# Cosine attention and a GELU feed-forward block on one core: attention passes of the next batch moved ahead of the w_in stage, with new filler portions and five more start-up spins

## The chip, the core and the metric

The kernel runs on one core of a Trainium2 chip. The metric is the device time of one launch in microseconds (us). A core has TensorE (PE, matrix multiplication; its weight loads are listed as PEld), VectorE (DVE), ScalarE (ACT), GpSimd (POOL) and SyncE (SP), which only issues transfers. Each takes its instructions in the order in which the kernel's code emits them, and semaphores tie the engines together. Matrix products land in PSUM, which has eight banks of 2 KB a partition, and have to be copied or consumed from there by DVE or ACT.

## What is computed

Attention on normalised q and k, for 8 batches of 12 heads, 448 positions and 64 channels, then two matrix products with a GELU between them:

```python
q_n = q / (norm(q) + 1e-6);  k_n = k / (norm(k) + 1e-6)
scores = q_n @ k_n.T / tau                     # tau = 0.1
attn = softmax(scores);      o = attn @ v      # per batch and head
x = o laid out as (8 * 448) x 768
out = gelu_exact(x @ w_in) @ w_out             # 768 -> 2048 -> 768
```

## The kernel before

**Stages.** For each batch b the program emits an attention stage, `attention(b, fill)` from line 600 on (batch 0 has its own, written out instruction by instruction, `attention_first`, line 411), and then the w_in stage `first(b)` (line 652): 96 matmuls `hp` (line 664) of 448 columns, each group of six followed by a GELU on ACT (line 699). The w_out product of a batch is not a stage of its own. It is cut into *fillers*, single matmuls of 384 columns (`second_pieces`, line 343), which are put between the parts of the next batch's attention. Sixteen fillers make a *piece*: they accumulate into one PSUM bank, and behind the last one DVE copies the bank to SBUF (`ot`, line 356); two pieces make a tile of the output that SyncE stores. A stage of an odd batch gets 96 fillers (six pieces), that of an even batch 128 (eight). What is left after the last batch runs at the end.

**Attention.** The 12 heads of a batch are three *quads* of four heads. A quad has seven key chunks, so a batch has 21 *passes*. A pass is four matmuls of 64 x 64 tiles that run side by side in the array (`st`, `scores`, line 246) and one exp on ACT over their result (`pt`, `exps`, line 253). `visit(b, pairs)` emits the next passes of batch b; its numbers say which of the three two-bank *pair* buffers of PSUM each pass uses. When a quad's seven passes are there, `both(g, p)` (line 325) emits its sums (`sm`, line 275, 16 matmuls), then DVE's chain that turns, adds, inverts and spreads the sums (lines 297, 309, 312, 314, 318), its values (`o`, line 289, 28 matmuls, into pair buffer p), and two multiplications on DVE that write x (line 323).

**Banks.** Two single PSUM banks, mm0 and mm1, serve everything else. `mm_tile` (line 99) hands out the bank that `turn` names and flips `turn`; each filler piece takes one that way at its first matmul. Sums ask with `aside=0`, which takes the bank that `turn` names without flipping it. A new owner of a bank waits until the old one's content has been read.

**Norms of later quads.** The squares of q and k run on GpSimd (line 156), their reduction `nq` on DVE (line 165), the logarithm and the root on ACT (lines 172 and 181), then a small addition on GpSimd, the reciprocal on DVE and the scaling of q and k on GpSimd (line 208). For batches from 1 on a DMA transposes the scaled q and k (line 220). `upto(f, n)` emits whatever of step f is not yet emitted up to number n. In an attention stage one reduction, for a quad of the next batch, is emitted between the first and the second quad's `both` (line 635); in batch 7 there is no such quad left.

**Order of a stage, batches 3 to 7.** `run()` emits the next portion of the fillers. With six portions, (16, 14, 16, 18, 16, 16) or (20, 18, 20, 22, 32, 16), the order is: fillers, 3 passes, fillers, 3, fillers, 3, fillers, 3, sums and values of quad 0, 2 passes, the reduction, fillers, 3 passes, sums and values of quad 1, 2 passes, fillers, sums and values of quad 2, 2 passes of the next batch. The w_in stage follows; its first two matmul groups use mm0 and mm1, the next four use pair buffers 0 and 1.

**Start.** `spin(n)` (line 406) emits n matmuls whose result nobody reads.

Of the kernel before, what the change touches and what calls it, by code (L numbers as in the profile page):

```python
# [16 lines left out]
def kernel(  # L17
# [18 lines left out]
    B, H, S, D = q.shape  # L36
# [163 lines left out]
    def scale(u, parts=None):  # L200
        g, s0, s1 = units[u]
        n, j = place[u]
        rn = rn_t[n][:, j]
        if g not in qkb_t:
            qkb_t[g] = qkbp.tile([128, 2, C, 2, D], BF16, tag="qkb", name=f"qkb{g}")
        qkb, t = qkb_t[g], qk_t[g]
        for eng, i in parts or ((nc.gpsimd, 0), (nc.gpsimd, 1)):
            eng.tensor_tensor(  # L208
                qkb[:, i, :, s0:s1].rearrange("p c s d -> p s c d"), t[:, i, s0:s1],
                rn[:, i].to_broadcast([128, s1 - s0, C, D]), ALU.mult)  # L210
# [3 lines left out]
    def transposes(u, i=None):  # L214
        g, s0, s1 = units[u]
        qkb = qkb_t[g]
        if g not in qkT_t:
            qkT_t[g] = qkTp.tile([128, 2, C, 128], BF16, tag="qkT", name=f"qkT{g}")
        if i is None:
            nc.sync.dma_start_transpose(out=qkT_t[g].rearrange("p i c s -> p (i c) s"),  # L220
                                        in_=qkb.rearrange("p i c s d -> p (i c s d)"))
            return
        tp = tp_t[u, i] = mm_tile(f"tp{u}_{i}", (128, C, 128), BF16)
        for c in range(C):
            nc.tensor.transpose(tp[64 * s0:64 * s1, c, :], qkb[:, i, c, s0:s1].rearrange("p s d -> p (s d)"), ident)  # L225
# [33 lines left out]
    def sums(g, chunks=range(C)):  # L259
        for c in chunks:  # L260
            if c == 0:
                bank_t[g, "sm"] = ps_acc.tile([128, 512], F32, tag="sm", name=f"sm{g}") if g < NQ else \
                    mm_tile(f"sm{g}", aside=0)
            for s in range(2):
                if g < NQ:
                    nc.tensor.matmul(bank_t[g, "sm"][64 * s:64 * (s + 1), :S],  # L266
                                     lhsT=ones2.rearrange("p a h r -> p (a h r)"), rhs=pt_t[g, s, c],
                                     start=(c == 0), stop=(c == C - 1), tile_position=(0, 64 * s))
                    continue

                half = 2
                for i in range(2) if c == half else ((c - (c > half)) % 2,):
                    r = 32 * (2 * s + i)
                    cols = slice(i * S // 2, (i + 1) * S // 2) if c == half else slice(0, S)
                    nc.tensor.matmul(bank_t[g, "sm"][r:r + 32, cols], lhsT=ones, rhs=pt_t[g, s, c][:, cols],  # L275
                                     start=(c < 2), stop=(c >= C - 2), tile_position=(0, r))

    def values(g, chunks=range(C), p=None):
        for c in chunks:
            if c == 0 and g < NQ:  # L280
                bank_t[g, 0] = ps_acc.tile([128, 512], F32, tag="o", name=f"o{g}_0")
                bank_t[g, 1] = mm_tile(f"o{g}_1")
            elif c == 0:
                o = pair(p, f"o{g}")
                bank_t[g, 0], bank_t[g, 1] = o[:, 0], o[:, 1]
            for s in range(2):
                for h in range(2):
                    rows, cols = slice(64 * h, 64 * (h + 1)), slice(64 * s, 64 * (s + 1))
                    nc.tensor.matmul(bank_t[g, h][cols, :S], lhsT=v_t[g][rows, s, c, :],  # L289
                                     rhs=pt_t[g, s, c][rows], start=(c == 0), stop=(c == C - 1),  # L290
                                     tile_position=(64 * h, 64 * s))
# [3 lines left out]
    def turned(g):  # L295
        tr = rcp.tile([128, NB, 32], F32, tag="tr", name=f"tr{g}")
        nc.vector.transpose(tr.rearrange("p b r -> p (b r)"), bank_t.pop((g, "sm"))[:, :S])  # L297
        bank_t[g, "tr"] = tr.rearrange("p b (k r) -> p k b r", k=2)

    def inverted(g):  # L300
        tr = bank_t.pop((g, "tr"))
        if g < NQ:
            su = tr[:, :, :, 0]
        else:


            for j in range(4):
                o = j ^ 1
                nc.vector.tensor_reduce(tr[32 * j:32 * (j + 1), :, :, 1], tr[32 * o:32 * (o + 1), :, :, 0:1],  # L309
                                        mybir.AxisListType.X, ALU.add)  # L310
            su = rcp.tile([128, 2, NB], F32, tag="su", name=f"su{g}")
            nc.vector.tensor_reduce(su, tr[:, :, :, 0:2], mybir.AxisListType.X, ALU.add)
        rc = bank_t[g, "rc"] = rcp.tile([128, 2, NB], F32, tag="rc", name=f"rc{g}")
        nc.vector.reciprocal(rc, su)

    def spread(g, h):
        rs = rcp.tile([128, NB, 32], F32, tag=f"rs{h}", name=f"rs{g}_{h}")
        nc.vector.transpose(rs, bank_t[g, "rc"][:, h].to_broadcast([128, NB, 32]))  # L318
        rs_t[g, h] = rs.rearrange("p b r -> p (b r)")

    def normalise(g, h):
        b, n = divmod(g, NQ)
        nc.vector.tensor_tensor(x_t[b][:, 2 * n + h, :], bank_t.pop((g, h))[:, :S], rs_t.pop((g, h)), ALU.mult)  # L323

    def both(g, p):
        sums(g)
        turned(g)
        inverted(g)
        spread(g, 0)
        spread(g, 1)  # L330
        values(g, p=p)
        normalise(g, 0)
        normalise(g, 1)
# [66 lines left out]
    def upto(f, n, last=None):  # L400
        last = {load_qk: NG, load_v: NV, root: len(groups), load_wi: NQ + 1, load_wo: 4}.get(f, NU)
        while done.get(f, 0) < min(n, last):
            done[f] = done.get(f, 0) + 1
            f(done[f] - 1)

    def spin(n):
        ps = ps_mm.tile([128, 512], F32, tag=f"mm{turn[0]}", name="spin")
        for _ in range(n):
            nc.tensor.matmul(ps[:, :S], lhsT=ident, rhs=blank, start=True, stop=True)  # L409

    def attention_first():
# [19 lines left out]
        reduce(2, Q)  # L431
        roots(1)
        scale(0, ((GP, 0),))
        spin(2)
        transposes(0, 1)
        square(2, ((AC, K),))
        inverses(1)
        spin(1)
        transposes(0, 0)
        square(3, ((AC, Q),))  # L440
        copies(0, 1)
# [2 lines left out]
        square(3, ((AC, K),))  # L444
        scale(1, ((GP, 1),))
        upto(load_qk, 5)
        spin(1)
        transposes(1, 0)
        reduce(2, K)
        scores(0, ((0, 0), (0, 1)))  # L450
# [8 lines left out]
        inverses(2)  # L459
        copies(1, 1)  # L460
        exps(0, ((0, 2), (0, 3)))
        spin(2)
        scores(0, ((0, 4), (0, 5)))
        scale(2, ((GP, 0),))
        reduce(3, Q)
# [127 lines left out]
    def visit(b, pairs):  # L593
        for p in pairs:
            n, c = passes[at.get(b, 0)]
            at[b] = at.get(b, 0) + 1
            scores(b * NQ + n, ((0, c), (1, c)), p)
            exps(b * NQ + n, ((0, c), (1, c)))

    def attention(b, fill):  # L600
        fill = list(fill)
        if len(fill) == 128:
            parts = iter((20, 18, 20, 22, 32, 16))
        else:
            parts = iter((20, 13, 14, 17, 16, 16) if b == 1 else (16, 14, 16, 18, 16, 16))

        def run():
            for _ in range(next(parts)):
                fill.pop(0)()

        x_t[b] = xp.tile([128, KD, S], BF16, tag="x", name=f"x{b}")
        g0, u = b * NQ, b * NQ + 1
        run()
        upto(scale, u + 3)
        upto(transposes, u + 3)
        if b == 1:
            upto(load_qk, g0 + NQ + 2)
            upto(square, u + 4)
        visit(b, (0, 1, 2))
        if b > 1:  # L620
            upto(scale, u + 4)
            upto(transposes, u + 4)
        run()
        visit(b, (0, 1, 2))
        run()
        upto(load_qk, g0 + NQ + 3)
        visit(b, (0, 1) if b <= 2 else (0, 1, 2))
        upto(square, u + 5)
        run()
        visit(b, (0, 1, 2))  # L630
        both(g0, 0)
        upto(load_v, b + 3)
        upto(load_qk, g0 + NQ + 4)
        visit(b, (1, 2))
        upto(reduce, u + 4 + (b > 1))
        run()
        visit(b, (1, 2, 0))
        both(g0 + 1, 1)
        visit(b, (2, 0))
        n = 2 * b + 5 + (b > 1)  # L640
        if n < len(groups):
            logs(n)
            roots(n)
        run()
        both(g0 + 2, 2)
        if n < len(groups):
            inverses(n)
            done[root] = n + 1
            if b > 1:
                visit(b + 1, (0, 1))  # L650

    def first(b):
        sb, hf = divmod(b, 2)
# [77 lines left out]
    fill = []  # L731
    for b in range(B):
# [12 lines left out]
        fill = [f for t, ni in todo if t not in tail for f in second_pieces(sb, t, ni)]  # L745
# [38 lines left out]
```

## Time and profile before

The time is 414.46 us, the median of three runs (414.1 to 420.34); the profiled execution has a span of 412.4 us.

| What | PE | PE weight loads | DVE | ACT | POOL |
|---|---|---|---|---|---|
| busy, us | 405.6 | 211.8 | 188.3 | 248.8 | 168.1 |
| share of the span | 98% | 51% | 46% | 60% | 41% |

Some costly groups of instructions, from the page:

| Group | Count | Mean ns of one |
|---|---|---|
| ACT exp `pt`, L253 | 168 | 916 |
| PE filler `op`, L352 | 864 | 326 |
| PE `hp`, L664 | 768 | 353 |
| PE scores `st`, L246 | 672 | 358 |
| PE values `o`, L289 | 672 | 352 |
| PE sums `sm`, L275 | 336 | 332 |
| DVE reduction `nq`, L165 | 30 | 1635 |
| DVE copy `ot`, L356 | 54 | 547 |

The page and the views name each row by line, engine and operation, and by the names of the tiles it writes and reads (`op<-wo,g`: writes op from wo and g). "x16" is a number of instructions merged into one row. Times in a timeline are us from the start of the span; brackets hold the idle time of that engine ahead of the row and what ended it. Consecutive matmuls overlap in the array, and their listed ends are modelled, so the distance from one start to the next says more than a listed length.

In the trace the attention stage of batch 3 takes 27.6 us (149.11 to 176.68), that of batch 4 32.8 us (194.85 to 227.63), and a w_in stage 18.2 us (176.68 to 194.85).

### The profile page before, as it was taken

The page shows a single profiled execution, that of the slowest core. Times are in us where ns is not written, and L with a number is a line of the kernel's source. Part 1 is how long each engine was busy: PE and PEld are TensorE (multiplying, and loading weights), DVE is VectorE, ACT ScalarE, POOL GpSimd, SP SyncE. Part 2 cuts the span into 40 slices and gives each one's busy share as a digit, 9 for nine tenths or more (in the row PEclk, how much of TensorE's full clock was granted, in tenths as well). Part 3 has the DMA queues.
Part 4 walks back from the last instruction along what each step waited for, and adds up shares of the span by engine and source line. Part 5 has one row for each costly group of instructions (what it writes and reads, how often), then busy time and mean ns, then how long its engine had stood idle before and what let it go on. Part 6 is the DMA issues. An engine that isn't in the chain of part 4 may idle for free.

```text
span 412.4 us, 8272 instructions
## 1 busy us (share of the span) xinstructions
PE 405.6 (98%) x3503; PEld 211.8 (51%) x3503; DVE 188.3 (46%) x380; ACT 248.8 (60%) x364; POOL 168.1 (41%) x117
## 2 busy tenths in 40 slices
PE   7999999999999999999999999999999999999996
PEld 3445555555555555555555555555555555555564
DVE  5785316931278222933158331773128611481021
ACT  6996696477556567665664658646665457754300
POOL 4996665094900928053720628227360233000000
PEclk9999999999999999999999999999999999999999
DMA  8999999852495507944496332965088120610033
GB/s 287 260 258 213 203 204 303 188 132 48 83 243 164 135 0 115 251 102 120 36 216 200 79 94 52 226 176 134 2 151 212 38 46 0 122 40 2 0 78 77
DMA packets 66484, 54.53 MB, mean 132 GB/s; under 512 B 38672, under 2 KB 62352, under 8 KB 66448
## 3 DMA queue, kind: packets, MB, share of 16 engines
q1 hardware_dynamic: 54464, 41.79, 39.7%
q0 software_dynamic: 11600, 11.80, 18.2%
q8 instruction: 27, 0.44, 0.4%
q10 hardware_dynamic: 384, 0.43, 0.3%
q14 instruction: 9, 0.07, 0.1%
HBM read 45.61 MB, written 11.01 MB: 137 GB/s over the span
## 4 chain that ended last, share of the span: by engine, by line
PE 96%; DMA 2%; SPq 1%; ACT 1%; issue 0%; DVE 0%
PE hp L664 35%; PE op L352 35%; PE st L246 10%; PE o L289 8%; PE sm L275 4%; DMA qk<-in_k_dram 2%; PE op L371 1%; PE sm L266 1%; PE tp L225 1%; SPq L129 1%; PE spin L409 0%; ACT sq L154 0%; ACT pt L253 0%; DVE last L374 0%; ACT root L178 0%
## 5 line engine op out<-in xcount | busy, mean ns | idle before, releaser
L253 ACT ACTIVATE pt<-st 128x896 bf16<-128x896 f32 x168 | 142.5, 916 | 65.4 <-PE st L246 65.1
L352 PE MATMUL op<-wo,g 128*128 128x384 bf16 x864 | 148.0, 326 | 0.0
L664 PE MATMUL hp<-x,wi 128*128 128x448 bf16 x768 | 146.9, 353 | 0.0
L352 PEld LDWEIGHTS <-g 128*128 128x128 bf16 x864 | 81.5, 98 | 62.2 <-issue 10.8
L664 PEld LDWEIGHTS <-wi 128*128 128x128 bf16 x768 | 74.4, 98 | 71.4 <-issue 3.0
L699 ACT ACTIVATE g<-hp 128x448 bf16<-128x448 f32 x128 | 65.5, 545 | 67.7 <-PE hp L664 67.5
L208 POOL TENSOR_TENSOR qkb<-qk,rn 128x896 bf16<-128x896 f32 (+1 forms) x50 | 80.3, 1632 | 41.1 <-DVE rn L192 41.1
L165 DVE TENSOR_REDUCE nq<-sq 128x28 f32<-128x1792 f32 (+2 forms) x30 | 48.7, 1635 | 51.4 <-POOL sq L156 47.7
L356 DVE COPY ot<-op 128x384 f32<-128x384 f32 x54 | 29.6, 547 | 88.2 <-PE op L352 86.1
L156 POOL TENSOR_TENSOR sq<-qk 128x1792 f32<-128x1792 f32 (+1 forms) x22 | 66.6, 3039 | 5.1 <-DMA qk<-in_k_dram 5.1
L190 POOL TENSOR_SCALAR se<-sr 128x28 f32<-128x28 f32 (+1 forms) x16 | 4.8, 298 | 124.4 <-ACT sr L181 124.2
L246 PE MATMUL st<-qkT 64*64 64x448 bf16 x672 | 47.8, 358 | 0.2 <-ACT pt L253 0.2
L289 PE MATMUL o<-pt,v 64*64 64x448 bf16 x672 | 37.2, 352 | 0.0
L192 DVE RECIPROCAL rn<-se 128x28 f32<-128x28 f32 (+2 forms) x20 | 7.1, 357 | 57.5 <-POOL se L190 57.3
L246 PEld LDWEIGHTS <-qkT 64*64 64x64 bf16 x672 | 18.3, 105 | 23.0 <-issue 14.8
L318 DVE STREAM_TRANSPOSE rs<-rc 128x448 f32<-128x448 f32 x48 | 28.2, 623 | 0.8
L323 DVE TENSOR_TENSOR x<-o,rs 128x448 bf16<-128x448 f32 x48 | 27.1, 598 | 0.3
L289 PEld LDWEIGHTS <-v 64*64 64x64 bf16 x672 | 17.8, 106 | 16.7 <-issue 8.1
L297 DVE STREAM_TRANSPOSE tr<-sm 128x448 f32<-128x448 f32 x24 | 15.5, 647 | 13.4 <-PE sm L275 11.1
L275 PE MATMUL sm<-pt,ones 128*32 128x448 bf16 (+1 forms) x336 | 17.8, 332 | 0.0
L309 DVE TENSOR_REDUCE tr<-tr 32x28 f32<-32x28 f32 x84 | 16.4, 196 | 1.6
L275 PEld LDWEIGHTS <-ones 128*32 128x32 bf16 x336 | 6.8, 96 | 9.0 <-issue 7.2
(43 smaller groups left out, 120.6 us busy)
## 6 DMA issues: line engine op xcount, KB each, us to landing
qk<-in_q_dram SPq DMA_DIRECT2D x23, 448.0 KB, 6.2
qk<-in_k_dram SPq DMA_DIRECT2D x23, 448.0 KB, 8.6
out_dram<-ot SPq DMA_DIRECT2D x48, 192.0 KB, 3.7
v<-in_v_dram POOLq DMA_DIRECT2D x7, 672.0 KB, 12.8
wo<-in_moe_w_out_dram POOLq DMA_DIRECT2D x4, 768.0 KB, 12.4
wi<-in_moe_w_in_dram POOLq DMA_DIRECT2D x4, 512.0 KB, 14.1
out_dram<-ot SPq DMA_DIRECT2D x12, 96.0 KB, 2.2
wi<-in_moe_w_in_dram POOLq DMA_DIRECT2D x4, 256.0 KB, 14.1
```

The source lines that it names most:

```text
L156: eng.tensor_tensor(sq[:, part], t[:, part], t[:, part], ALU.mult)
L165: nc.vector.tensor_reduce(nq[:, part], sq[:, part], mybir.AxisListType.X, ALU.add)
L208: eng.tensor_tensor(qkb[:, i, :, s0:s1].rearrange("p c s d -> p s c d"), t[:, i, s0:s1], rn[:, i].to_broadcast([128, s1 - s0, C, D]), ALU. ...
L246: nc.tensor.matmul(st[cols, n, :S], lhsT=qkT[rows, 1, c, cols], rhs=qkT[rows, 0, :, cols], start=True, stop=True, tile_position=(64 * s, 6 ...
L253: nc.scalar.activation(pt[:, :m], st[:, :m, :S], AF.Exp, scale=inv_tau)
L275: nc.tensor.matmul(bank_t[g, "sm"][r:r + 32, cols], lhsT=ones, rhs=pt_t[g, s, c][:, cols], start=(c < 2), stop=(c >= C - 2), tile_position ...
L289: nc.tensor.matmul(bank_t[g, h][cols, :S], lhsT=v_t[g][rows, s, c, :], rhs=pt_t[g, s, c][rows], start=(c == 0), stop=(c == C - 1), tile_po ...
L318: nc.vector.transpose(rs, bank_t[g, "rc"][:, h].to_broadcast([128, NB, 32]))
L352: nc.tensor.matmul(ps[:, :NH], lhsT=g_t[sb][:, kf, t * 128:(t + 1) * 128], rhs=wo[:, kf, ni * NH:(ni + 1) * NH], start=(kf == 0), stop=(kf ...
L356: nc.vector.tensor_copy(ot[:, ni * NH:(ni + 1) * NH], ps[:, :NH])
L664: nc.tensor.matmul(hps[m], lhsT=wi[:, kd, m * 128:(m + 1) * 128], rhs=x_t[b][:, kd, :], start=(kd == 0), stop=(kd == KD - 1))
L699: nc.scalar.activation(g_t[sb][:, m, hf * S:(hf + 1) * S], hps.pop(m), AF.Gelu)
```

## The change

From batch 3 on, five passes of a batch (not two) are emitted in the stage before it: three ahead of the sums and values of the last quad, two behind them. They are to give ACT work ahead of the w_in stage and to take three passes out of the following attention stage, whose fillers are then handed out in five portions instead of six. Batches 1 and 2 keep their portions. In the first batch five more spins are emitted, at four places, where PE would be waiting for other engines.

```diff
@@ attention_first
         scale(0, ((GP, 0),))
-        spin(2)
+        spin(4)
         transposes(0, 1)
...
         inverses(1)
-        spin(1)
+        spin(2)
         transposes(0, 0)
...
         upto(load_qk, 5)
-        spin(1)
+        spin(2)
         transposes(1, 0)
...
         exps(0, ((0, 2), (0, 3)))
-        spin(2)
+        spin(3)
         scores(0, ((0, 4), (0, 5)))
@@ attention(b, fill)
-        if len(fill) == 128:
-            parts = iter((20, 18, 20, 22, 32, 16))
+        if b <= 2:
+            parts = iter((20, 13, 14, 17, 16, 16) if b == 1 else (20, 18, 20, 22, 32, 16))
         else:
-            parts = iter((20, 13, 14, 17, 16, 16) if b == 1 else (16, 14, 16, 18, 16, 16))
+            parts = iter((26, 26, 26, 25, 25) if len(fill) == 128 else (20, 19, 19, 19, 19))
...
         upto(load_qk, g0 + NQ + 3)
-        visit(b, (0, 1) if b <= 2 else (0, 1, 2))
+        if b <= 2:
+            visit(b, (0, 1))
+            run()
         upto(square, u + 5)
-        run()
         visit(b, (0, 1, 2))
         both(g0, 0)
...
         run()
+        if 1 < b < B - 1:
+            visit(b + 1, (2, 0, 1))
         both(g0 + 2, 2)
         if n < len(groups):
             inverses(n)
             done[root] = n + 1
-            if b > 1:
-                visit(b + 1, (0, 1))
+        if 1 < b < B - 1:
+            visit(b + 1, (0, 1))
```

## The prediction

> **What bounds the kernel now.** I read the page first: the busy shares, then the chain that ended last.
>
> ```profile
> PE 405.6 (98%) x3503; PEld 211.8 (51%) x3503; DVE 188.3 (46%) x380; ACT 248.8 (60%) x364; POOL 168.1 (41%) x117
> ...
> PE 96%; DMA 2%; SPq 1%; ACT 1%; issue 0%; DVE 0%
> ```
>
> TensorE (PE) is 98% busy and is 96% of the chain; no other engine comes near. A busy share can hide waits, so I next read the timeline of PE for the batch with a short filler list (batch 3) and took start-to-start distances.
>
> ```profile
> 162.00 0.76 PE L246 MATMUL st<-qkT 64*64 64x448 bf16 x12
> 162.69 0.85 PE L275 MATMUL sm<-pt,ones 128*32 128x448 bf16 x16
> 163.46 1.52 PE L289 MATMUL o<-pt,v 64*64 64x448 bf16 x28
> 164.81 0.59 PE L246 MATMUL st<-qkT 64*64 64x448 bf16 x8
> 165.33 2.77 PE L352 MATMUL op<-wo,g 128*128 128x384 bf16 x16
> 168.04 0.76 PE L246 MATMUL st<-qkT 64*64 64x448 bf16 x12
> 168.73 0.85 PE L275 MATMUL sm<-pt,ones 128*32 128x448 bf16 x16
> ```
>
> Columns: start, length, instruction, count. Three passes (st x12) take 0.69 us to the next start, sums 0.77 to 0.78, values 1.35, two passes 0.52. Filler blocks (op) of 14, 16, 18 and 20 take 2.38, 2.70, 3.03 and 3.35 us: 0.1625 us a matmul and 0.10 us once per block. No block takes longer than its like anywhere from batch 3 on: PE waits for nothing there. So the time is PE's work plus whatever waits the change brings. Where could it wait? The next view is the timeline of VectorE (DVE) beside the same stretch.
>
> ```profile
> 162.10 0.56 DVE L356 COPY ot<-op 128x384 f32<-128x384 f32 x1 [2.04 <-PE op L352]
> 163.59 0.65 DVE L297 STREAM_TRANSPOSE tr<-sm 128x448 f32<-128x448 f32 x1 [0.93 <-PE sm L275]
> 164.27 0.82 DVE L309 TENSOR_REDUCE tr<-tr 32x28 f32<-32x28 f32 x4
> ...
> 166.83 1.11 DVE L323 TENSOR_TENSOR x<-o,rs 128x448 bf16<-128x448 f32 x2
> 167.87 2.00 DVE L165 TENSOR_REDUCE nq<-sq 128x28 f32<-128x1792 f32 x1
> 169.79 0.54 DVE L356 COPY ot<-op 128x384 f32<-128x384 f32 x1
> 170.26 0.63 DVE L297 STREAM_TRANSPOSE tr<-sm 128x448 f32<-128x448 f32 x1
> ```
>
> After the first quad's sums DVE works without a pause: the quad's chain (transpose to x) ends 5.18 us after the sums began at 162.69, then the reduce of the squares, and only then the copy that empties a filler piece: 7.10 us after the sums' start, done at 7.64. That piece's last matmul was over at about 168.0; its copy came 1.8 us late, because DVE takes its instructions in program order. It does no harm here, since the sums of the second quad (168.73) go into the bank of the piece before, which the copy at 162.10 had emptied.
>
> **What the Trainium skill says.** "Perfetto Trace Analysis", Identifying the Most-Contended Engine: matmul busy time doesn't tell how close PE is to its peak. The trace agrees: a filler matmul is listed at some 326 ns, but the starts are 162.5 ns apart, hence my use of starts. "TensorE: Matmul & The Clock Gate", Back-to-back issue gap: N/2.4 + 2.5 ns at full clock; that is 162.5 ns for 384 columns and 189 for 448, both as in the trace (hp: 18.17 us for 96). Same page, Architectural detail: VectorE and ScalarE are strictly first in, first out; the late copy above agrees. Same page, What's actually happening: after an idle window of about 3.4 us the PE clock falls to half. In the trace the spins' starts are 373 ns apart until 5.2 us and 189 ns after, and the granted clock stays full to the end of the matmuls.
>
> **The change part by part.**
>
> 1. Spins: five more matmuls at four places, 0.19 us each (5.43 to 5.62 in the trace), 0.95 us if all lay on the path. At line 434 two more (0.38) fall into an idle 0.81 before the transposes, which wait for GpSimd. At 447 one falls into an idle 0.20, again before GpSimd's scaling. At 462 the scores at 13.71 wait for an exp, with 0.15 idle; three spins from 13.01 and 0.10 for the change of shape end at 13.68. At 438 one has no room and pushes a transpose by some 0.06, which the next wait for GpSimd (0.20) takes up. I take 0; bounds 0 to 0.95.
>
> 2. Passes moved. The count stays 21 a batch. From batch 3 to 7 the block of passes between fillers goes and its two neighbouring filler parts join: one block less, 0.10 each, -0.50 us. Three passes stand ahead of the last quad's sums in batches 2 to 6: a block of 0.69, of which 0.56 is work taken from the next batch and 0.13 the change of tile shape. It replaces the block that went, so only batch 2 gains one (+0.13) and batch 7 loses one (-0.13). Sum -0.5 us. ScalarE's exps: five in a row need 5 x 0.81 = 4.1 us while PE is busy for 3.3 (0.69 + 0.78 + 1.35 + 0.48) and then 1.5 us on two other banks in the w_in stage, and the pair buffers are asked for in the order already used around the first quad, where nothing waits. Cost 0. Inputs: the third quad's transposed q and k must be there 13.9 us into the stage; the DMA transpose issued at 156.27 landed at 160.28, 11.2 us in. Cost 0.
>
> 3. Filler parts, and here I see a new wait. Fillers come as pieces of 16 matmuls, alternating between two banks; a piece's first matmul waits for the copy of the piece two before. Sums take the bank that the next piece would take: that of the piece before the current one. Before, the first quad's sums stand at filler 64 (short list) or 80 (long), both whole pieces, so the copy of the last piece goes ahead of the DVE chain. After, they stand at 20+19+19 = 58 and 26+26+26 = 78: a piece is cut, it ends just behind the sums, and its copy falls behind DVE's chain and the reduce, at 7.10 to 7.64 us after the sums' start.
>
> Short list (batches 3, 5): piece 4 ends 6 matmuls behind. The next quad's sums stand at filler 77, in piece 5, so they want piece 4's bank. They are due after 0.78 + 1.35 + 0.52 + (19 x 0.1625 + 0.10 = 3.19) + 0.69 = 6.53 us; the bank is free at 7.64 + 0.05 for the hand-over (from an exp's end to the scores at 13.71: 0.05). Wait 1.16 us.
>
> Long list (batches 4, 6): piece 5 ends 2 behind, piece 6 16 later, and piece 7 wants piece 5's bank. It is due after 0.78 + 1.35 + 0.52 + 18 x 0.1625 = 5.58 us. In batch 4 before, where PE's timeline has the first quad's sums at 211.03, DVE's has the reduce in the same place:
>
> ```profile
> 216.22 2.00 DVE L165 TENSOR_REDUCE nq<-sq 128x28 f32<-128x1792 f32 x1
> 218.14 0.54 DVE L356 COPY ot<-op 128x384 f32<-128x384 f32 x1
> ```
>
> The copy begins 7.11 after the sums and ends at 7.65; wait 7.65 + 0.05 - 5.58 = 2.12 us. Behind the waiting matmul stand all of PE's later matmuls, and nothing else can fill in, since PE takes them in order. Batch 7 has no reduce (no quad left to prepare): its copy ends at 5.18 + 0.54 = 5.7, before 6.53. Batch 2 keeps its old parts. After the wait DVE catches up: the next copies end at least 0.8 us before their banks are asked for.
>
> Sum of the waits: 2 x 1.16 + 2 x 2.12 = 6.6 us. With -0.5 and the spins at 0: 414.46 + 6.1 = **420.5 us**.
>
> **Rivals.** No wait: if the copy came ahead of the reduce or the banks alternated otherwise, only -0.5 would be left: 413.9 us, not slower than before. For it speaks that PE waits nowhere now; against it, the copy at 169.79 behind the reduce, and the sums at 168.73 not waiting for that copy, which is just the bank rule above. Chance 0.13. More waits: in batches 2 and 7, or for spins on the path (+0.95) and one DMA transpose late by 2 us, since transposes landed up to 8.8 us after issue: 423.5 us, chance 0.07. Clock: a wait of 2.1 us that counts as an idle window would bring 3.4 us at half speed, an estimate by the clock-gate page, 1.7 us each in four places: 427 us; against it, the wait is shorter than that window. Chance 0.05. My forecast has 0.75.
>
> **How the numbers follow.** The forecast alone moves little: DVE's order is measured twice, so its waits may be off by some 0.3 us each, and spins by up to 0.95. The range of 417.5 to 423.0 holds it, one of the four waits missing or halved, and part of the third case; left out are the first rival, the clock and the rest of the third, some 0.2. Slower by over 2% is over 422.8 us: 0.10. Faster by 2% would be under 406.2, which no case reaches: 0.01. Within 2%: 0.89.
>
> **What would show it.** In PE's timeline of batches 3 and 5 the passes ahead of the second quad's sums last about 1.2 us longer; in 4 and 6 the filler block of 25 takes 6.3 instead of 4.16 us; among the waits PE appears behind DVE's copy, four times, 6 to 7 us in all. The reduce of line 165 stands right before each late copy. Batch 7 shows none. I am wrong if these blocks have their usual lengths, or if the wait is for an exp or a DMA.

## The result, and the profile after

The changed kernel takes 421.83 us (median of six executions), the kernel before beside it 414.75. The ratio is 1.0173, with a 95% interval of 1.0152 to 1.0194: slower by some 7 us, within the stated range of 417.5 to 423.0, and 1.3 us over the forecast of 420.5. The ratio leaves out two executions of the kernel before, of 420.34 and 420.95 us; later ones like them, of kernels that wait for no copy, have a mean granted clock of 0.983 to 0.987, and no trace shows where they lost it.

The page of the changed kernel, busy shares and the chain that ended last:

```profile
PE 408.5 (97%) x3508; PEld 213.7 (51%) x3508; DVE 188.1 (45%) x380; ACT 249.0 (59%) x364; POOL 168.1 (40%) x117
...
PE 92%; DVE 6%; issue 1%; DVEq 0%
```

The span grew by 8.0 us (412.4 to 420.4), but PE's busy time only by 2.9. PE's work is nearly the same, and DVE, which had 0% of the chain, has 6% of it now. The timeline of PE for batch 3 (columns as before; the brackets give the idle time ahead of the row and what ended it):

```profile
164.54 3.26 PE L352 MATMUL op<-wo,g 128*128 128x384 bf16 x19
167.73 0.76 PE L246 MATMUL st<-qkT 64*64 64x448 bf16 x12
169.60 0.85 PE L275 MATMUL sm<-pt,ones 128*32 128x448 bf16 x16 [1.11 <-DVE ot L356]
```

and for batch 4:

```profile
214.61 3.10 PE L352 MATMUL op<-wo,g 128*128 128x384 bf16 x18
219.67 1.30 PE L352 MATMUL op<-wo,g 128*128 128x384 bf16 x7 [1.96 <-DVE ot L356]
```

In batch 3 the second quad's sums start 1.87 us after the passes ahead of them instead of 0.69: a wait of 1.18 us for the copy `ot`. In batch 4 the filler block of 25 breaks after its 18th matmul and lasts 6.29 us instead of 4.17: a wait of 2.12. DVE's timeline of batch 3 shows what stood ahead of that copy:

```profile
162.80 0.65 DVE L297 STREAM_TRANSPOSE tr<-sm 128x448 f32<-128x448 f32 x1 [2.55 <-PE sm L275]
...
166.05 1.12 DVE L323 TENSOR_TENSOR x<-o,rs 128x448 bf16<-128x448 f32 x2
167.09 2.00 DVE L165 TENSOR_REDUCE nq<-sq 128x28 f32<-128x1792 f32 x1
169.01 0.54 DVE L356 COPY ot<-op 128x384 f32<-128x384 f32 x1
```

The sums began at 161.90; the copy starts 7.11 us later and ends at 169.55, and PE's next sums start at 169.60. Cutting the trace at the starts of the attention stages (the view of given stretches: start and end, length, then the busy time and number of instructions of PE, PEld, DVE, ACT and POOL, then the granted PE clock, that is, the share of full speed at which PE was allowed to run, and last the DMA share and GB/s) gives the whole account:

```profile
97.77:150.09 52.32, 52.32 (x462) 27.42 (x461) 24.70 (x47) 33.74 (x48) 20.82 (x12) 1.00 0.50 123
150.09:196.91 46.82, 45.71 (x410) 23.85 (x408) 22.28 (x44) 29.71 (x43) 20.82 (x12) 1.00 0.54 130
196.91:249.91 53.00, 51.04 (x442) 26.97 (x440) 23.30 (x46) 29.71 (x43) 20.82 (x12) 1.00 0.51 122
249.91:296.73 46.82, 45.71 (x410) 23.85 (x409) 22.27 (x44) 29.71 (x43) 20.82 (x12) 1.00 0.54 130
296.73:351.26 54.53, 52.57 (x441) 27.21 (x440) 21.25 (x45) 29.71 (x43) 17.69 (x11) 0.97 0.39 85
351.26:395.83 44.57, 44.57 (x389) 23.25 (x388) 15.91 (x40) 24.97 (x36) 3.62 (x3) 1.00 0.17 38
```

Before, the same stretches (attention and w_in stage of batches 2 to 7) are 51.58, 45.74, 50.95, 45.74, 50.95 and 45.37 us long, and PE is busy through all of each. The "predicted" column adds up the terms of the prediction.

| Batch | Before, us | After, us | Measured | Predicted |
|---|---|---|---|---|
| up to batch 2's start | 97.53 | 97.77 | +0.24 | 0 |
| 2 | 51.58 | 52.32 | +0.74 | +0.69 |
| 3 | 45.74 | 46.82 | +1.08 | +1.06 |
| 4 | 50.95 | 53.00 | +2.05 | +2.02 |
| 5 | 45.74 | 46.82 | +1.08 | +1.06 |
| 6 | 50.95 | 54.53 | +3.58 | +2.02 |
| 7 | 45.37 | 44.57 | -0.80 | -0.79 |

Five stages are within 0.05 us of the prediction. Batch 6 takes 1.53 us more than batch 4, which has the same work, and a mean granted clock of 0.97. These short stretches around its wait show why:

```profile
317.51:320.92 3.41, 1.45 (x12) 0.72 (x14) 2.38 (x3) 0.00 (x0) 0.00 (x0) 1.00 1.01 356
320.92:324.33 3.41, 3.41 (x40) 1.19 (x36) 0.91 (x3) 2.54 (x3) 0.00 (x0) 0.50 0.51 144
```

For 3.41 us behind the wait PE ran at half its clock. Four of the six executions have a mean granted clock of 0.994 or 0.995, which is about one such stretch (half of 3.41 us is 0.4% of 420), and take 421.79 to 422.21 us; the two at 1.0 take 420.66 and 420.96. The waits by themselves therefore give about the forecast, and a clock drop in most executions adds 1.2 us. Of the six, only the profiled one has a trace; for the other five the number of drops is read from the mean clock.

### The profile page after: what moved, and what is told of

It reads as the page before. It is cut to its first block, busy times and chain, and to the rows that moved or that the text cites. A ratio compares the mean times of both kernels' runs of the same rounds, so it can differ in the third digit from the quotient of the medians.

```text
span 420.4 us, 8269 instructions
## 1 busy us (share of the span) xinstructions
PE 408.5 (97%) x3508; PEld 213.7 (51%) x3508; DVE 188.1 (45%) x380; ACT 249.0 (59%) x364; POOL 168.1 (40%) x117
## 2 busy tenths in 40 slices
DMA packets 66484, 54.53 MB, mean 130 GB/s; under 512 B 38672, under 2 KB 62352, under 8 KB 66448
## 4 chain that ended last, share of the span: by engine, by line
PE 92%; DVE 6%; issue 1%; DVEq 0%
PE hp L667 35%; PE op L352 31%; PE st L246 9%; PE o L289 7%; PE sm L275 4%; PE spin L409 2%; DVE nq L165 2%; PE op L371 1%; PE sm L266 1%; PE tp L225 1%; DVE tr L309 1%; DVE x L323 1%; DVE rs L318 1%; DVE tr L297 1%; DVE ot L356 0%
```

## The experiments

The theory is that PE waits for filler copies that the new portions put behind DVE's chain and the reduction, and that the longer wait can set off a clock drop. Rival P says that the passes moved ahead cost the time themselves. Rival S puts a good part of it at the start, on the spins. A piece is called cut where the sums stand inside it, and whole where they stand at its end.

### The spins alone

```diff
 # the kernel before
-        spin(2)
+        spin(4)
         transposes(0, 1)
...
 # and the three other places of the change
```

> The kernel before with the five added spins alone. Theory (the added time is the wait for a late copy, plus a clock drop that the wait sets off): the spins cost 0 to 0.4 us, so 414.4 to 414.9; 0.4 where the clock comes up late and the 24 spins reach past the scaling that the first transposes wait for. Rival S (a good part of the added 7 us lies at the start): 415.5 or more.

Measured: 414.68 us, ratio 1.0005 (0.9995 to 1.0014). A cost of up to 0.6 us is all that this allows; it can't be told from none. Rival S falls. The trace of the changed kernel shows how the spins can get onto the path: there the clock became full at 6.89 us, not 5.22, so the first 24 spins were slower, and the transposes started behind them at 9.33, while GpSimd's scaling had ended at 8.67. Two spins fewer would have freed PE 0.38 us earlier. In the trace with the spins alone the clock became full at 5.68, and the transposes followed the scaling (8.76) at 8.82, so there the first spins cost nothing. That execution is the slowest of its fifteen (417.81 us); it lost its time later on, where PE waited 1.17 us for a copy on DVE and 1.72 us for an exp on ACT, which had itself waited 2.28 us for a transfer of k.

### Cut pieces in the kernel before

```diff
 # the kernel before, in attention
-        if len(fill) == 128:
+        if b > 2:
+            parts = iter((20, 18, 20, 20, 25, 25) if len(fill) == 128
+                         else (16, 14, 16, 12, 19, 19))
+        elif len(fill) == 128:
             parts = iter((20, 18, 20, 22, 32, 16))
```

> The kernel before with the filler portions alone changed, from batch 3 on: (16, 14, 16, 12, 19, 19) and (20, 18, 20, 20, 25, 25), so that the sums stand at fillers 58 and 77, or 78 and 103, as in the changed kernel. Passes and spins as before. Theory: the same four waits, 2 x 1.17 and 2 x 2.12 us, in all 6.6: 421.0 us, and 1.7 more in an execution with a clock drop. Rival P: 414.5, since the passes are where they were.

Measured: 421.98 us (median of four), ratio 1.0180 (1.0160 to 1.0201). The profiled execution took 420.9 and shows the four waits without a clock drop; the others have clocks of 0.995 and 0.996 and take 421.7 to 422.9. From the view of the waits (us in total, times, longest us):

```profile
PE op L352 <- DVE ot L356: 3.9, 2, 2.0
PE sm L275 <- DVE ot L356: 2.2, 2, 1.1
```

The stages of batches 3 to 6 grew by 1.15, 2.12, 1.14 and 2.12 us, 6.5 together; those of 2 and 7 did not change. Nothing but the portions differs from the kernel before, so moving the passes isn't needed for the loss: rival P falls as its cause.

### The reduction behind the copies

```diff
 # the changed kernel
-        upto(reduce, u + 4 + (b > 1))
+        if b <= 2:
+            upto(reduce, u + 4 + (b > 1))
         run()
+        upto(reduce, u + 4 + (b > 1))
```

> The changed kernel with the reduction of the squares emitted behind the filler portion that follows the first quad, so that it stands behind the copies on VectorE, for batches 3 to 6. The cut pieces stay. Theory: the copy ends 5.72 us after the sums began; no wait in batches 3 and 5 (due at 6.53), 0.2 us in 4 and 6 (due at 5.58); no clock drop; 414.3 to 415.0 us. Rival P, or a rival in which the cut pieces cost by themselves: about 421.

Measured: 414.24 us, ratio 0.9997 (0.9986 to 1.0008). The cut pieces, the passes ahead and the new spins are all still there; only the place of the reduction in DVE's order is another. DVE's timeline of batch 4:

```profile
214.91 1.12 DVE L323 TENSOR_TENSOR x<-o,rs 128x448 bf16<-128x448 f32 x2
215.95 1.14 DVE L356 COPY ot<-op 128x384 f32<-128x384 f32 x2
217.01 2.01 DVE L165 TENSOR_REDUCE nq<-sq 128x28 f32<-128x1792 f32 x1
219.36 0.65 DVE L297 STREAM_TRANSPOSE tr<-sm 128x448 f32<-128x448 f32 x1 [0.34 <-PE sm L275]
```

The copies now end before the reduction, which ends before the next sums are done. PE's timeline of the same stretch:

```profile
213.40 4.44 PE L352 MATMUL op<-wo,g 128*128 128x384 bf16 x25
217.77 0.76 PE L246 MATMUL st<-qkT 64*64 64x448 bf16 x12
```

The filler block of 25 takes 4.37 us, against 4.17 without a wait: the 0.2 that was expected. So the 7 us are the reduction's place in DVE's queue, given cut pieces.

### Whole pieces in the changed kernel

```diff
 # the changed kernel
-            parts = iter((26, 26, 26, 25, 25) if len(fill) == 128 else (20, 19, 19, 19, 19))
+            parts = iter((27, 27, 26, 32, 16) if len(fill) == 128 else (22, 21, 21, 16, 16))
```

> The changed kernel, passes ahead and spins kept, with filler portions (27, 27, 26, 32, 16) and (22, 21, 21, 16, 16): the first two quads' sums stand at fillers 80 and 112, or 64 and 80, whole pieces as before. Theory: no wait of PE for a copy and no clock drop, 413.9 to 414.5 us. Rival P (five passes ahead cost the time, by exps or by more changes of tile shape): about 421, as they are all still there.

Measured: 414.66 us, ratio 1.0011 (1.0000 to 1.0022). The waits for copies and the clock drops are gone, and with them the 7 us; but it isn't faster than the kernel before, and lies just above what was expected. The stages of batches 2 to 7 sum to 290.31 us, against 290.33 before, where the prediction had 0.5 less. The long stages are 0.07 shorter, the short ones 0.10 longer. There, in batch 3, the passes ahead of the last quad's sums take 0.90 us instead of 0.69. The third of them starts at 175.10, right behind DVE's writing of the second quad's x, which frees the pair buffer that it uses:

```profile
173.93 1.11 DVE L323 TENSOR_TENSOR x<-o,rs 128x448 bf16<-128x448 f32 x2
174.97 0.54 DVE L356 COPY ot<-op 128x384 f32<-128x384 f32 x1
```

With 16 fillers between the two quads instead of 19 the pass comes 0.5 us earlier, and DVE, which still has the reduction ahead of the second quad's chain, is not through. The rest of the time above the kernel before is at the start, where this kernel has the new spins; executions differ there by more than that, so it isn't settled.

### One list cut at a time

```diff
 # the changed kernel: the long list cut, the short one whole
-            parts = iter((26, 26, 26, 25, 25) if len(fill) == 128 else (20, 19, 19, 19, 19))
+            parts = iter((26, 26, 26, 25, 25) if len(fill) == 128 else (22, 21, 21, 16, 16))
```

> The changed kernel with the portions of the short list whole, (22, 21, 21, 16, 16), and the long list's cut as in the change. Theory: the two waits of 2.12 us in batches 4 and 6 remain, 4.2 us; batches 3 and 5 as in the run with whole pieces: about 418.8 us, and 1.6 more in the executions with a clock drop, which should be some 6 in 10.

```diff
 # the changed kernel: the short list cut, the long one whole
-            parts = iter((26, 26, 26, 25, 25) if len(fill) == 128 else (20, 19, 19, 19, 19))
+            parts = iter((27, 27, 26, 32, 16) if len(fill) == 128 else (20, 19, 19, 19, 19))
```

> The changed kernel with the portions of the long list whole, (27, 27, 26, 32, 16), and the short list's cut as in the change. Theory: the two waits of 1.2 us in batches 3 and 5 remain, 2.4 us: about 416.6 us, and no clock drop in any execution, since a window can hold no more than 1.3 us of idle.

Measured, both about as expected: the long list cut, 420.5 us, ratio 1.0140 (1.0119 to 1.0162); the short list cut, 416.33, ratio 1.0047 (1.0028 to 1.0066). The long list's two waits of 2.12 us come with a clock of 0.994 to 0.996 in three of four executions (420.4 to 420.7) and 1.0 in the fourth (418.96), the short list's two of 1.2 us with 0.998 or more in all four. The drop goes with the longer wait. In the profiled execution with the long list cut it fell in batch 4:

```profile
215.98:219.40 3.42, 1.46 (x10) 0.78 (x8) 3.42 (x5) 0.00 (x0) 0.00 (x0) 1.00 1.15 289
219.40:222.81 3.41, 3.41 (x23) 1.12 (x24) 0.14 (x1) 0.95 (x2) 0.00 (x0) 0.50 1.06 405
```

### Two reductions

```diff
 # the changed kernel
         upto(reduce, u + 4 + (b > 1))
+        if 2 < b < B - 1:
+            reduce(u + 4)
```

> The changed kernel with the reduction of the squares emitted twice in a row in batches 3 to 6 (the second writes the same values): 1.92 us more of VectorE ahead of the late copies. Theory of the wait: each of the four waits grows by 1.92 us, to 3.1 and 4.0, 14.3 in all, so without clock drops about 428.7 us. Theory of the clock (it drops for one 3.41 us window when a window of that length, running free of the program, holds some 2 us or more of idle PE): three to four drops of 1.6 us each, in all 433 to 435. Rival (the drop in the changed kernel was chance, or needs a wholly idle window): no more than one drop on average, under 431.

Measured: the four executions took 431.84, 433.69, 438.87 and 439.18 us. The ratio, 1.0445 (1.0414 to 1.0476), is of the first two: 432.6 us against 414.18, just under the expected 433 to 435, and over the 431 of the rival. The other two have a clock of 0.968, far more half-clock time than one drop per wait makes, and where they had it stays open. The profiled execution is the one of 431.84. Its waits behind `ot` are 3.17 and 4.02 us, against 1.11 and 1.96:

```profile
171.62 0.85 PE L275 MATMUL sm<-pt,ones 128*32 128x448 bf16 x16 [3.17 <-DVE ot L356]
...
223.74 1.86 PE L352 MATMUL op<-wo,g 128*128 128x384 bf16 x7 [4.02 <-DVE ot L356]
```

Each grew by 2.06, a little more than the 1.92 that was expected for the second reduction, so time added on DVE comes out about one to one on PE. The clock dropped after both of the long waits and after neither of the 3.2 us ones, two drops where three or four were expected; the other execution in the comparison has a clock of 0.987, about three drops, and 433.69 us. The stretches of 3.41 us around the wait of batch 3 and that of batch 4 show the difference:

```profile
169.72:173.13 3.41, 1.51 (x32) 0.83 (x35) 2.46 (x3) 0.94 (x2) 0.00 (x0) 1.00 1.15 293
173.13:176.55 3.42, 3.42 (x43) 1.89 (x32) 3.24 (x11) 2.16 (x4) 0.05 (x1) 1.00 1.01 375
220.91:224.33 3.42, 0.59 (x4) 0.38 (x4) 3.21 (x4) 0.00 (x0) 0.00 (x0) 1.00 1.07 376
224.33:227.74 3.41, 3.41 (x33) 1.13 (x30) 0.00 (x0) 1.56 (x2) 0.00 (x0) 0.50 0.63 177
```

The wait of 3.2 us in batch 3 falls across two windows and leaves 1.51 us of PE time in the emptier one: the clock stays full. In batch 5 the two windows have 1.81 and 1.86 us, and it stays full too.

### The reduction late, and the long list whole at the first quad

```diff
 # the kernel with the reduction behind the copies, and the spins of the kernel before
-            parts = iter((26, 26, 26, 25, 25) if len(fill) == 128 else (20, 19, 19, 19, 19))
+            parts = iter((27, 27, 26, 24, 24) if len(fill) == 128 else (20, 19, 19, 19, 19))
```

> The changed kernel with the spins of the kernel before, the reduction behind the filler portion, and the long list's portions (27, 27, 26, 24, 24). Theory: no wait of PE from batch 2 on; against the kernel before only the saved changes of tile shape are left, -0.35 us in the stages of batches 2 to 7: 413.8 us, at the limit of what can be told from 414.2. Rival P (the passes ahead cost something of their own): over 414.5.

Measured: 413.85 us, ratio 0.9986 (0.9971 to 1.0002). It takes what is good in the change and avoids the rest. The stages of batches 2 to 7 sum to 290.00 us against 290.33, so the trace has 0.33 less, where 0.35 was expected; by the times of whole executions it can't be told from the kernel before. Rival P, over 414.5, falls here too.

## Why the prediction was right

**What bounds the kernel** held: PE's work stayed, and each microsecond of its waiting came out as one of the total.

**The filler parts and the new wait** were the heart of it. The working gave 1.16 us for the short list and 2.12 for the long; the traces have 1.18 and 2.12. The copy came 7.11 us after the sums, where 7.10 and 7.11 stood in the trace before, and the hand-over took 0.05. Four waits, not in batches 2 and 7, as forecast. That the bank rule and DVE's order cause it is shown from three sides: the cut alone brings it (421.98), either whole pieces or a later reduction take it away (414.66, 414.24), and a longer DVE queue lengthens it (3.17 and 4.02 us).

**The passes moved** were forecast at -0.5 us and give -0.33 in the best case. Batch 2 (+0.74 for 0.69) and batch 7 (-0.80 for -0.79) are right; batches 3 to 6 save 0.07 each where a joined block was to save 0.10. In the timeline the two passes ahead of the w_in stage take 0.52 us instead of 0.48, which is about the missing 0.03; why they take longer is open. The skill's page "TensorEngine Tiling (Array Packing)", Key Properties, says that a change of tiling mode drains PE. The traces fit this: 0.10 us is lost on leaving a filler block and 0.13 us on leaving a block of passes.

**The spins** were taken at 0 with bounds to 0.95. The step left out that the first 24 spins run at half clock for as long as the clock takes to come up, and in the profiled execution that was 1.67 us longer than before. The first w_in matmul came 0.42 us later (32.55 against 32.13), but that can't be put down to the spins: with cut pieces in the kernel before, which has the old spins, it came at 32.48. Over many executions the cost lies between nothing and 0.6.

**The clock** is the step that failed: a drop was put at nothing in the forecast. The rival got 0.05, "against it, the wait is shorter than that window". The wait needn't be as long as the window. Drops followed windows of 3.41 us in which the view lists PE as busy for 0.59, 0.94, 1.45 and 1.46 us, and none followed windows with 1.51 (two reductions), 1.60 (cut pieces in the kernel before, batch 4), 1.81 and more. The end of the program, where PE runs out of work, agrees: the clock fell after a last window with 1.42 us (cut pieces in the kernel before) and stayed full after one with 1.62 (the last run above). So in these traces a wait of 2.1 us drops the clock when it falls wholly, or nearly so, into one window, and not when it is divided between two; the window's place against the program differs from execution to execution. In the changed kernel the wait of batch 4 was divided (2.61 and 2.26 us of PE time in its windows), that of batch 6 was not (1.45). That is why an execution has one drop or none, not four, and why the rival's 427 us was too much while the forecast was 1.3 too little. The price of a drop was estimated at 1.7 us; batch 6 against batch 4 has 1.53 (54.53 against 53.00, where both took 50.95 in the kernel before). That the result still lies in the range is partly luck: the range's upper part was set aside for other cases, and the clock was expressly left out of it.

## What to carry to other kernels

When portions of filler work are rearranged around a stage, it's not enough to count the work between two points: look where each accumulation *ends*, because its copy goes to the other engine's queue there and behind whatever that queue already holds. With two alternating banks, end an accumulation just ahead of a long run on the copying engine, never just behind its start, or emit a long, patient instruction (here the reduction) after the copies. And a short wait can cost more than itself: here a wait of 2.1 us could bring 3.41 us of half clock, another 1.5 us.

## What the runs showed of the hardware that was not expected

The half clock didn't need a window that was idle throughout: one with some 57% of idle PE was enough. In the traces of this case the granted clock changes at multiples of 3.413 us from where it first became full (6.89 and 320.92 us in the changed kernel, 92 windows apart). It fell for one window after a window in which PE was listed as busy for 1.46 us or less, and stayed full after 1.51 us or more, so the limit lies between 43% and 44% of the window; each time in the course of the program it came back after one window of dense matmuls. The skill's page "TensorE: Matmul & The Clock Gate", What's actually happening, speaks of an idle window; the runs agree with its length and with the window running free of the program, but here a window counted in which PE was listed as busy for 43% of the time. These windows are few, and the listed ends of matmuls are modelled, so the limit is one for this mixture of matmuls.
